# Softcap attention feeding a max-of-two-projections layer: the matmul order inside g, the place of quad 0's first attention-times-V, and the place of w1 - w2

## The chip, the cores and the metric

The kernel runs on one core of one Trainium2 chip. The time is the device time of one execution in microseconds (us), taken as the median over several executions. Before the change it is 378.27 us (13 runs, 377.13 to 380.69).

The core has four engines that matter here, each with its own in-order instruction stream: TensorE (PE) does matrix products and writes them into PSUM banks; VectorE (DVE) copies results out of PSUM and does elementwise work; ScalarE (ACT) does tanh and exp; GpSimd (POOL) does casts, one multiply, and starts some transfers. SyncE (SP) only issues transfers. An instruction that waits holds up everything behind it on its own engine.

## The reference: what is computed

Inputs are q, k and v of shape (8 batches, 12 heads, 448 positions, 64), and the weights w1, w2 (768 x 1024) and w_out (1024 x 768), all in float32.

```python
scores = scale * q @ k.T            # per batch and head, scale = 1/8
scores = cap * tanh(scores / cap)   # cap = 30
attn   = exp(scores - max) / (sum(exp(scores - max)) + 1e-9)
x      = attn @ v                   # heads side by side: 3584 tokens x 768
out    = maximum(x @ w1, x @ w2) @ w_out
```

## The kernel before, in words

**Algebra.** Because |scores| is at most 30, the row maximum is not subtracted. The maximum of the two projections is rewritten: max(x w1, x w2) = x w2 + relu(x (w1 - w2)). So the kernel forms `wd` = w1 - w2 (`wd_sb`) and `wm` = w2 w_out (`wm_sb`) once, and each batch then needs g = relu(x wd) and out = x wm + g w_out. All matrix products are in bf16.

**Attention, in quads.** A pair is two heads of one batch, and there are 48 pairs. A quad t is two consecutive pairs i = 2t and 2t + 1, so there are 24 quads and three quads make a batch. For each quad: `scores(t, p)` (lines 277 to 298) does the products of k and q of part p = 0..3 on PE, into one of two double-bank `s` tiles, followed by tanh on ACT; `ex(t, p)` (line 300) is the exp on ACT; `pv(t, ab)` (line 330) is attention times v for one of the two pairs: seven matmuls into the one `pv` bank, then a copy to `u` by DVE (line 356). `pv(t, 1)` also adds up the exponentials into the `ss` bank (lines 345 and 352), which DVE copies to `st` and SP sends out for the reciprocals. The bank pool of `pv` has one buffer, so a `pv` can't start before the `u` copy of the one before is done. Later come `invert` (reciprocal, line 368), `spread` (transfer of the reciprocals to all partitions, `rec_b`, line 376) and `normalize` (POOL multiplies `u` by `rec_b` into `xT`, line 388). `xT` has six chunks per batch, one per pair; chunks 4 and 5 are from the batch's last quad.

**Setting up.** `transposes(i)` turns the early k and q on PE, and DVE copies them (line 264). `cast(nc.vector, 0, "v")` puts group 0's v into bf16 `vp` on DVE (lines 151 and 155). The rows of w2 are turned on PE (line 221) and multiplied by w_out (line 232). `subtract(c)` (line 214) makes chunk c of `wd_sb` on DVE from a chunk of w1 (`w1_in`, three buffers in the `osb` pool, loaded by `load_w1`) and w2.

**The filler.** Everything that is not attention runs as generators in the list `fill_q`: each `yield` follows one matmul, and `F(n)` lets the first generators advance n matmuls. The main loop over quads (line 534 on) strews `F(n)` between the attention steps, so PE always has work between two score products. The order on every engine is written out by hand in this way: the kernel turns the scheduler off with `tc.manual_schedule()`, and the order of the emission is the order of the instructions. After the last quad the rest of the filler runs alone.

**One batch of the layer** is the generator `moe(b)` (line 397 on). The first part computes g in eight blocks f = 0..7 of 128 columns; each block is six matmuls (chunks c = 0..5 of `xT`, line 405) into one bank of the `mm` pool, which has two banks, and then one relu copy by DVE (line 410). The second part is the output in tiles of 128 tokens and half rows: six matmuls with `wm_sb` (line 418), eight with `wo_sb` (line 421), and a copy to `osb` (line 425). Both parts take turns on the same two `mm` banks. In the kernel before, blocks 0 and 1 are done together: chunks 0 to 3 of block 0, chunks 0 to 3 of block 1, then chunks 4 and 5 of block 0, then chunks 4 and 5 of block 1. Blocks 2 to 7 follow one at a time.

Of the kernel before, what the change touches and what calls it, by code (L numbers as in the profile page):

```python
# [10 lines left out]
def kernel(  # L11
# [11 lines left out]
    nc = tc.nc  # L23
# [9 lines left out]
    P = 128  # L33
# [277 lines left out]
    def add(t, ab, step):  # L311

        if t < NS or t >= NQ:
            return
        if t not in esum:
            esum[t] = att.tile([P, 4, S], bf16, name="esum")
        d = esum[t][:, 2 * ab : 2 * ab + 2, :]
        if step == 2:

            r = slice(64 * ab, 64 * ab + 64)  # L320
            d = esum[t][r, ab::2, :]
            nc.vector.tensor_add(d, d, expo[t, 2][r, :, :])  # L322
        elif step == 0:
            nc.vector.tensor_add(d, e_of(t, ab, 1 if ab else 0), e_of(t, ab, 2 if ab else 1))  # L324
        else:
            nc.vector.tensor_add(d, d, e_of(t, ab, 0 if ab else 2))  # L326
# [3 lines left out]
    def pv(t, ab):  # L330


        i = 2 * t + ab
        g, n = divmod(i, L)
        ps = pv_psum.tile([P, 512], f32, name="pv")
        for j in range(NJ):
            for h in range(2):
                r = slice(64 * h, 64 * h + 64)
                nc.tensor.matmul(  # L339
                    ps[r, :S], vp[g % 2][:, 2 * n + h, j, :], e_of(t, ab, j)[:, h, :], start=(j == 0), stop=False  # L340
                )
        if ab:
            ss = pv_psum.tile([P, 512], f32, name="ss")
            for m in range(2 if t < NS else 0):
                nc.tensor.matmul(
                    ss[64 * m : 64 * m + 64, :S], ones2, expo[t, 2][:, m, :], start=True, stop=False
                )
            nj = NJ if t < NS else 1
            for j in range(nj):
                for m in range(4):  # L350
                    x = e_of(t, m // 2, j)[:, m % 2, :] if t < NS else esum[t][:, m, :]
                    nc.tensor.matmul(ss[32 * m : 32 * m + 32, :S], ones, x, start=(t >= NS), stop=(j == nj - 1))  # L352
        nc.tensor.matmul(ps[:, :S], vl[g % 2][:, n, :], expo[t, 2][:, ab, :], start=False, stop=True)  # L353
        if ab == 0:
            U[t] = upool.tile([P, 2, S], f32, name="u", bufs=4)
        nc.vector.tensor_copy(U[t][:, ab, :], ps[:, :S])  # L356
        if ab:
            st = upool.tile([P, S], f32, name="st", bufs=1)
            nc.vector.tensor_copy(st, ss[:, :S])

            sums[t] = xpool.tile([32, 56], f32, name="sums")
            nc.sync.dma_start(
                out=sums[t], in_=st.rearrange("(m p) (a c) -> m p a c", p=32, a=8)[:, 0, :, :]
            )
# [28 lines left out]
    def moe(b):  # L393
        if b % 2 == 0:
            gT[b // 2] = xpool.tile([P, FC, 2 * S], bf16, name="gT", bufs=1)
        g, x = gT[b // 2], xT[b // 2]
        cs = slice((b % 2) * S, (b % 2 + 1) * S)

        psg = {f: mm_psum.tile([P, 512], f32, name="mm") for f in range(2)}
        order = [(f, c) for cc in (range(4), range(4, KC)) for f in range(2) for c in cc]  # L400
        order += [(f, c) for f in range(2, FC) for c in range(KC)]
        for f, c in order:
            if f not in psg:
                psg[f] = mm_psum.tile([P, 512], f32, name="mm")
            nc.tensor.matmul(  # L405
                psg[f][:, :S], wd_sb[:, c, f * P : (f + 1) * P], x[:, c, cs], start=(c == 0), stop=(c == KC - 1)
            )
            yield
            if c == KC - 1:
                nc.vector.tensor_relu(g[:, f, cs], psg[f][:, :S])  # L410
        for t in range(3) if b % 2 == 0 else range(3, 7):
            osb = opool.tile([P, DF], f32, name="osb")[:, :DM]
            ts = slice(t * P, (t + 1) * P)
            for half in range(2):
                hs = slice(half * (DM // 2), (half + 1) * (DM // 2))
                ps = mm_psum.tile([P, 512], f32, name="mm")
                for c in range(KC):
                    nc.tensor.matmul(ps[:, : DM // 2], x[:, c, ts], wm_sb[:, c, hs], start=(c == 0), stop=False)  # L418
                    yield
                for f in range(FC):  # L420
                    nc.tensor.matmul(  # L421
                        ps[:, : DM // 2], g[:, f, ts], wo_sb[:, f, hs], start=False, stop=(f == FC - 1)
                    )
                    yield
                nc.vector.tensor_copy(osb[:, hs], ps[:, : DM // 2])  # L425
                if b == B - 1 and t == 6:
                    o = out[b * S : b * S + NJ * P, hs].rearrange("(p j) n -> p j n", j=NJ)
                    nc.sync.dma_start(out=o[:, NJ - 1, :], in_=osb[:, hs])
            if b == B - 1 and t == 6:
                continue  # L430
            wide = b * NP >= NT * L
            if t == 3:
                for n in range(2):
                    o = out[(b - 1 + n) * S : (b + n) * S, :]
                    to = o[NJ * P : S, :] if wide else o.rearrange("(r j) n -> r j n", j=R7)[:, R7 - 1, :]
                    nc.sync.dma_start(out=to, in_=osb[64 * n : 64 * n + 64, :])
            else:
                j = t if t < 3 else t - 4
                o = out[b * S : (b + 1) * S, :]
                if wide:  # L440
                    nc.sync.dma_start(out=o[: NJ * P, :].rearrange("(p j) n -> p j n", j=NJ)[:, j, :], in_=osb)
                else:
                    o = o.rearrange("(r j) n -> r j n", j=R7)
                    for n in range(2):
                        nc.sync.dma_start(out=o[:, 2 * j + n, :], in_=osb[64 * n : 64 * n + 64, :])
# [3 lines left out]
    def F(n):  # L449
        while n > 0 and fill_q:  # L450
            try:
                next(fill_q[0])
                n -= 1
            except StopIteration:
                fill_q.pop(0)
# [78 lines left out]
    for t in range(NQ):  # L534
        i = 2 * t
        more = t + 1 < NQ
        more8 = 1 if t >= 8 and more else 0
        weights(i)
        if t % 3 == 2 and t > 5:
            fill_q.append(moe(t // 3 - 1))  # L540
        if more:
            scores(t + 1, 0)
        ex(t, 3)
        F(2)
        add(t, 0, 1)
        F(2)
        if i + 3 < NT * L:
            transposes(i + 3)
        if t == 0:
            cast(nc.vector, 0, "v")  # L550
        F(4 + more8 if more else 0)
        if t == 4:
            normalize(t - 2, 0)
            normalize(t - 2, 1)
        if t in crosses:
            cross(crosses[t])
        if t > 4:
            spread(t - 2)
        extra(i)
        F(5 + 2 * more8 if more else 3)  # L560
        if more:
            scores(t + 1, 1)
            ex(t + 1, 0)
        pv(t, 0)
        F(4)
        add(t, 1, 0)
        F(3 + more8 if more else 4)
        F(3 if more else 0)
        if 3 <= i < 3 + KC:
            subtract(i - 3)  # L570
        if t > 4:
            normalize(t - 2, 0)
            normalize(t - 2, 1)
        if more:
            scores(t + 1, 2)
            ex(t + 1, 1)
        weights(i + 1)
        if t == 4:
            fill_q.append(moe(0))
        if i + 4 < NT * L:  # L580
            transposes(i + 4)
        add(t, 0, 2)
        F(2 + more8 if more else 2)
        add(t, 1, 2)
        F(4 + more8 if more else 3)
        add(t, 1, 1)
        F(2 if more else 8)
        if 1 < t < 4:
            spread(t - 2)
        if t > 2:  # L590
            invert(t - 1)
        extra(i + 1)
        F(2 + more8 if more else 0)
        if more:
            scores(t + 1, 3)
            ex(t + 1, 2)
        if t == 3:
            spread(t - 1)
        pv(t, 1)
        F(4)  # L600
        if more:
            add(t + 1, 0, 0)
        F(3 if more else 0)
        if 0 < t < 3:
            invert(t - 1)
        if 1 < t < 4:
            normalize(t - 2, 0)
            normalize(t - 2, 1)
        if 3 <= i + 1 < 3 + KC:
            subtract(i - 2)  # L610
    F(6)
    spread(NQ - 2)
    F(10)
# [43 lines left out]
```

## Time and profile before

| | |
|---|---|
| median of 13 runs | 378.27 us (377.13 to 380.69) |
| the profiled execution's own time | 377.69 us |
| its span on the core | 375.9 us |
| PE busy | 343.3 us, 91% |
| ACT busy | 281.7 us, 75% |
| DVE busy | 231.0 us, 61% |
| POOL busy | 160.9 us, 43% |
| matmuls of g (line 405) | 384 |
| relu copies (line 410) | 64, 38.8 us in all |

The span is the time from the first to the last instruction; the 1.8 us by which the execution's own time is longer lie around it. In the lists of instructions below, the columns are the start in us from the span's start, the length in us, the engine, the line, the operation with its output and inputs, the shape, and how many instructions are merged; in square brackets stands the idle time of the engine just before, with what ended it. In the lists of waits, the columns are the engine and line that waited, what it waited for, the total in us, how often, and the longest.

### The profile page before, as it was taken

The numbers are of one execution on the slowest core, as the hardware profiler recorded it, in microseconds if no ns is written. First come the engines' busy times: TensorE is split into PE (matmuls) and PEld (weight loads), VectorE is DVE, ScalarE is ACT, GpSimd is POOL, SyncE is SP. The second block draws the span as 40 slices with busy tenths as digits, with TensorE's granted clock in tenths as the row PEclk, the third lists the DMA queues.
The fourth block names the chain that finished last, engine by engine and source line by source line (L and its number), as shares of the span: only waits on it lengthen the run. The fifth ranks groups of instructions, "written<-read, shape, count | busy, mean of one in ns | idle before, by whom it ended". The sixth has DMA issues, their size and how long they took to land.

```text
span 375.9 us, 6501 instructions
## 1 busy us (share of the span) xinstructions
PE 343.3 (91%) x2454; PEld 164.5 (44%) x2454; DVE 231.0 (61%) x389; ACT 281.7 (75%) x265; POOL 160.9 (43%) x197
## 2 busy tenths in 40 slices
PE   4667897899999999989999999989998999999996
PEld 2224344444444444434453445434443445455563
DVE  4163567576776776767775767577666968433421
ACT  4979998798999999987998899978996892000000
POOL 4770079592664356308433942384415222220000
PEclk9999999999999999999999999999999999999999
DMA  7999899758799969688799889999866034512022
GB/s 245 340 234 216 319 263 277 138 141 210 191 234 234 246 179 242 189 206 235 203 224 242 219 213 228 218 269 212 235 151 188 8 91 136 143 44 84 0 85 84
DMA packets 101200, 71.56 MB, mean 190 GB/s; under 512 B 56496, under 2 KB 96176, under 8 KB 101168
## 3 DMA queue, kind: packets, MB, share of 16 engines
q1 hardware_dynamic: 99216, 67.99, 68.7%
q0 software_dynamic: 1952, 3.15, 4.5%
q8 instruction: 19, 0.31, 0.3%
q14 instruction: 13, 0.11, 0.1%
HBM read 53.48 MB, written 11.18 MB: 172 GB/s over the span
## 4 chain that ended last, share of the span: by engine, by line
PE 71%; DVE 13%; ACT 11%; issue 2%; DMA 2%; SPq 0%; POOL 0%; DVEq 0%; ACTq 0%
PE mm L421 17%; PE mm L405 16%; PE mm L418 13%; PE pv L339 8%; PE s L295 7%; ACT expo L303 5%; ACT tanh L296 5%; PE pv L353 3%; PE ss L352 2%; PE mm L232 2%; DMA kr<-in_k_dram 2%; PE s L290 2%; DVE gT L410 2%; DVE u L356 1%; DVE esum L324 1%
## 5 line engine op out<-in xcount | busy, mean ns | idle before, releaser
L303 ACT ACTIVATE expo<-tanh 128x1792 bf16<-128x1792 bf16 (+1 forms) x96 | 144.8, 1509 | 0.1
L296 ACT ACTIVATE tanh<-s 128x896 bf16<-128x896 f32 x144 | 124.2, 914 | 24.6 <-PE s L295 23.1
L388 POOL TENSOR_TENSOR xT<-u,rec_b 128x448 bf16<-128x448 f32 x48 | 60.9, 1289 | 132.1 <-DMA rec_b<-rec_d 101.6
L405 PE MATMUL mm<-xT,wd_sb 128*128 128x448 bf16 x384 | 80.9, 352 | 7.6 <-DVE gT L410 5.5
L421 PE MATMUL mm<-wo_sb,gT 128*128 128x384 bf16 x448 | 85.3, 326 | 0.0
L356 DVE COPY u<-pv 128x448 f32<-128x448 f32 x48 | 30.0, 625 | 75.8 <-PE pv L353 75.8
L418 PE MATMUL mm<-wm_sb,xT 128*128 128x384 bf16 x336 | 66.9, 326 | 0.2 <-DVE gT L410 0.2
L405 PEld LDWEIGHTS <-wd_sb 128*128 128x128 bf16 x384 | 36.9, 98 | 45.2 <-issue 14.2
L421 PEld LDWEIGHTS <-gT 128*128 128x128 bf16 x448 | 43.4, 98 | 30.0 <-issue 2.2
L295 PE MATMUL s<-qkT 64*128 64x448 bf16 x288 | 43.5, 370 | 7.9 <-ACT tanh L298 3.1
L425 DVE COPY osb<-mm 128x384 f32<-128x384 f32 x56 | 31.0, 553 | 28.6 <-PE mm L421 28.2
L410 DVE TENSOR_SCALAR gT<-mm 128x448 bf16<-128x448 f32 x64 | 38.8, 618 | 14.7 <-PE mm L405 14.4
L418 PEld LDWEIGHTS <-xT 128*128 128x128 bf16 x336 | 32.5, 98 | 23.5 <-issue 1.9
L339 PE MATMUL pv<-expo,vp 128*64 128x448 bf16 x288 | 37.5, 365 | 3.2 <-DVE vp L151 3.2
L326 DVE TENSOR_TENSOR esum<-esum,expo 128x896 bf16<-128x896 bf16 x38 | 30.7, 808 | 1.7
L324 DVE TENSOR_TENSOR esum<-expo 128x896 bf16<-128x896 bf16 x38 | 28.0, 736 | 0.0
L322 DVE TENSOR_TENSOR esum<-esum,expo 64x896 bf16<-64x896 bf16 x38 | 26.9, 708 | 0.7
L298 ACT ACTIVATE tanh<-s 128x896 bf16<-128x896 f32 x24 | 22.0, 916 | 5.7 <-PE s L290 5.1
L295 PEld LDWEIGHTS <-qkT 64*128 64x128 bf16 x288 | 9.8, 95 | 33.5 <-issue 29.0
L339 PEld LDWEIGHTS <-vp 128*64 128x64 bf16 x288 | 12.4, 109 | 24.7 <-issue 15.5
L232 PE MATMUL mm<-wo_sb,w2T 128*128 128x384 bf16 x96 | 18.4, 326 | 4.5 <-DVE qkT L264 4.5
L151 POOL CAST vp<-vr 64x576 bf16<-64x576 f32 x12 | 8.9, 738 | 20.5 <-PE s L295 17.6
(59 smaller groups left out, 251.9 us busy)
## 6 DMA issues: line engine op xcount, KB each, us to landing
rec_b<-rec_d SPq DMA_DIRECT2D x48, 224.0 KB
kr<-in_k_dram SPq DMA_DIRECT2D x12, 576.0 KB
qr<-in_q_dram SPq DMA_DIRECT2D x12, 576.0 KB
vr<-in_v_dram SPq DMA_DIRECT2D x12, 576.0 KB
out_dram<-osb SPq DMA_DIRECT2D x17, 384.0 KB
out_dram<-osb SPq DMA_DIRECT2D x22, 192.0 KB
osb<-in_moe_w_dram SPq DMA_DIRECT2D x6, 512.0 KB
vr<-in_v_dram SPq DMA_DIRECT2D x4, 672.0 KB
```

The source lines that it names most:

```text
L295: nc.tensor.matmul(s[:, h, :S], k0[r, j * P : (j + 1) * P], qTn[r, :])
L296: nc.scalar.activation(tanh[t, p][:, 2 * m : 2 * m + 2, :], s[:, :, :S], AF.Tanh, scale=scale / cap)
L303: nc.scalar.activation(expo[t, p], tanh[t, p][:, 0:n, :], AF.Exp, scale=float(cap))
L324: nc.vector.tensor_add(d, e_of(t, ab, 1 if ab else 0), e_of(t, ab, 2 if ab else 1))
L339: nc.tensor.matmul(ps[r, :S], vp[g % 2][:, 2 * n + h, j, :], e_of(t, ab, j)[:, h, :], start=(j == 0), stop=False)
L356: nc.vector.tensor_copy(U[t][:, ab, :], ps[:, :S])
L388: eng.tensor_mul(xT[b // 2][:, hp, cs], U[t][:, ab, :], rec[t][:, ab, :])
L405: nc.tensor.matmul(psg[f][:, :S], wd_sb[:, c, f * P : (f + 1) * P], x[:, c, cs], start=(c == 0), stop=(c == KC - 1))
L410: nc.vector.tensor_relu(g[:, f, cs], psg[f][:, :S])
L418: nc.tensor.matmul(ps[:, : DM // 2], x[:, c, ts], wm_sb[:, c, hs], start=(c == 0), stop=False)
L421: nc.tensor.matmul(ps[:, : DM // 2], g[:, f, ts], wo_sb[:, f, hs], start=False, stop=(f == FC - 1))
L425: nc.vector.tensor_copy(osb[:, hs], ps[:, : DM // 2])
```

## The change

Three edits.

1. In `moe`, the eight blocks of g are each done in one go: six matmuls, then the relu copy, for f = 0 to 7. The pairing of blocks 0 and 1 is gone.
2. `pv(0, 0)`, the first attention times v of all, is put off: it no longer stands after part 1 of quad 1's scores but after part 3, just ahead of `pv(0, 1)`. All other quads keep their order.
3. Three of the six `subtract` calls (chunks 0, 2 and 4) move from the end of quads 1, 2 and 3 into the next quad, behind its first scores, an exp and two filler matmuls.

```diff
-        psg = {f: mm_psum.tile([P, 512], f32, name="mm") for f in range(2)}
-        order = [(f, c) for cc in (range(4), range(4, KC)) for f in range(2) for c in cc]
-        order += [(f, c) for f in range(2, FC) for c in range(KC)]
-        for f, c in order:
-            if f not in psg:
-                psg[f] = mm_psum.tile([P, 512], f32, name="mm")
-            nc.tensor.matmul(
-                psg[f][:, :S], wd_sb[:, c, f * P : (f + 1) * P], x[:, c, cs], start=(c == 0), stop=(c == KC - 1)
-            )
-            yield
-            if c == KC - 1:
-                nc.vector.tensor_relu(g[:, f, cs], psg[f][:, :S])
+        for f in range(FC):
+            ps = mm_psum.tile([P, 512], f32, name="mm")
+            for c in range(KC):
+                nc.tensor.matmul(
+                    ps[:, :S], wd_sb[:, c, f * P : (f + 1) * P], x[:, c, cs], start=(c == 0), stop=(c == KC - 1)
+                )
+                yield
+            nc.vector.tensor_relu(g[:, f, cs], ps[:, :S])
...
         ex(t, 3)
         F(2)
+        if 3 < i <= 3 + KC:
+            subtract(i - 4)
         add(t, 0, 1)
...
             scores(t + 1, 1)
             ex(t + 1, 0)
-        pv(t, 0)
+        if t > 0:
+            pv(t, 0)
         F(4)
...
             scores(t + 1, 3)
             ex(t + 1, 2)
+        if t == 0:
+            pv(t, 0)
         if t == 3:
             spread(t - 1)
         pv(t, 1)
...
             normalize(t - 2, 0)
             normalize(t - 2, 1)
-        if 3 <= i + 1 < 3 + KC:
-            subtract(i - 2)
```

## The prediction

> **What bounds the kernel now.** I read the 40 slices and the chain first, then the waits of PE, then PE's and DVE's instructions around each place that the change touches.
>
> ```profile
> PE   4667897899999999989999999989998999999996
> ACT  4979998798999999987998899978996892000000
> ...
> PE 71%; DVE 13%; ACT 11%; issue 2%; DMA 2%; SPq 0%; POOL 0%; DVEq 0%; ACTq 0%
> ```
>
> A slice is 9.4 us. From 80 us on PE is full, ACT nearly so up to about 310 us, and then PE works alone. So a PE wait after 80 us costs time, provided ACT, which PE feeds, has idle time of its own there. PE's waits after 80 us (total, times, longest):
>
> ```profile
> PE mm L405 <- DVE gT L410: 5.5, 9, 1.4
> PE mm L405 <- DVE osb L425: 1.4, 3, 1.0
> PE mm L405 <- DVE wm_sb L237: 0.6, 1, 0.6
> PE s L295 <- ACT tanh L298: 0.5, 1, 0.5
> PE s L295 <- ACT tanh L296: 0.5, 2, 0.3
> ```
>
> Nearly all are matmuls of g (L405) waiting for DVE to empty an `mm` bank. The same list for ACT has 16.9 us of waits for PE's scores after 80 us (L296 14.3, L298 2.6), so ACT follows when PE gets faster.
>
> The last batch shows the wait alone, with nothing else running:
>
> ```profile
> 344.48 2.49 PE L405 MATMUL mm<-xT,wd_sb 128*128 128x448 bf16 x12
> 347.30 6.97 PE L405 MATMUL mm<-xT,wd_sb 128*128 128x448 bf16 x36 [0.34 <-DVE gT L410]
> ```
>
> The 36 matmuls take 6.97 us with a last length of 0.35, so they start every (6.97 - 0.35)/35 = 0.189 us. Twelve should bring block 2 to 344.48 + 12 x 0.189 = 346.75; it starts at 347.30. The price is 0.55, not the 0.34 of idle time: a matmul's drawn length of 0.352 hides 0.16 of each wait. Over the 13 waits for banks the price is 5.5 + 1.4 + 0.6 + 13 x 0.16 = 9.6 us.
>
> **Edit 1: blocks of g in one go.** No instruction is added or removed. Before, blocks 0 and 1 end only two matmuls apart (0.38 us), and block 2 needs the bank of block 0 just then, while its relu copy takes 0.62. After, block 2 comes six matmuls (1.13 us) behind block 0's end. That this distance suffices on a free DVE is seen in the 36: blocks 2 to 7 follow each other at six matmuls with no wait. Also, block 1 asks for its bank two matmuls (0.38) later, so the waits for `osb` and `wm_sb` shrink by up to 0.38.
>
> The largest wait, in batch 2 (PE, then DVE):
>
> ```profile
> 162.95 0.92 PE L405 MATMUL mm<-xT,wd_sb 128*128 128x448 bf16 x4
> 164.12 1.29 PE L405 MATMUL mm<-xT,wd_sb 128*128 128x448 bf16 x6 [0.25 <-DVE osb L425]
> 167.02 0.54 PE L405 MATMUL mm<-xT,wd_sb 128*128 128x448 bf16 x2
> 168.97 1.10 PE L405 MATMUL mm<-xT,wd_sb 128*128 128x448 bf16 x5 [1.40 <-DVE gT L410]
> ```
>
> ```profile
> 167.22 0.62 DVE L356 COPY u<-pv 128x448 f32<-128x448 f32 x1 [2.10 <-PE pv L353]
> 167.76 0.61 DVE L359 COPY st<-ss 128x448 f32<-128x448 f32 x1
> 168.30 1.15 DVE L410 TENSOR_SCALAR gT<-mm 128x448 bf16<-128x448 f32 x2
> ```
>
> Both relu copies stand behind `u` and `st` of an attention step. After, block 0 ends near 164.1, and in DVE's new order its copy stands ahead of `u`, in the 2.10 us of idle time. Block 1 starts at 164.12 as before (the bank comes free then) but has only four matmuls left to do ahead of the scores, not six: 0.38 gained. Block 2 then follows at 167.4 - 0.38 = 167.02 rather than 168.97: 1.95 in all. Block 3 needs block 1's copy, third in DVE's queue, done at 168.5 and wanted at 168.6.
>
> Worked likewise from each batch's rows:
> - Batch 0: block 1 still waits for `wm_sb` to 83.87; block 2 at 83.87 + 1.13 = 85.00, its copy done at 85.06 (behind an `esum`), against 85.88: 0.82.
> - Batch 1: 124.92 becomes 124.35 (copy in the place of an `esum` at 123.72): 0.57.
> - Batch 3: `osb` wait (0.21) and gT wait (0.34) both go; 203.42 becomes 202.55: 0.87.
> - Batch 4: block 2 from 248.03 to 246.80, but block 1's copy now stands behind an `esum` of 1.37 (the neighbours without POOL beside them take 0.61), so block 3 waits to about 248.45 against 249.16: 0.71 is left. This is what is late next.
> - Batch 5: the waits of 1.21 and 0.46 become one, since block 2's copy still stands behind two slow `esum` (1.02 and 1.37); block 4 at 287.25 against 288.04: 0.79.
> - Batches 6 and 7: 0.55 each.
>
> Sum 6.8 us. The upper bound is all 9.6. The lower is the two last batches alone in full and half of the other 5.7, if ACT or DVE holds PE instead: 1.1 + 2.85 = 3.95.
>
> **Edit 2: pv(0, 0) put off.**
>
> ```profile
> 23.92 1.33 PE L339 MATMUL pv<-expo,vp 128*64 128x448 bf16 x5 [1.83 <-DVE vp L151]
> 25.53 0.95 PE L290 MATMUL s<-qkT 128*128 128x448 bf16 x2
> 28.22 0.76 PE L339 MATMUL pv<-expo,vp 128*64 128x448 bf16 x6
> ```
>
> ```profile
> 26.58 0.92 ACT L298 ACTIVATE tanh<-s 128x896 bf16<-128x896 f32 x1 [2.44 <-PE s L290]
> ```
>
> PE waits for DVE's casts of v, and the scores behind that (L290) leave ACT idle for 2.44 us. After, these scores need only a free `s` bank (21.7), so tanh follows the exp at 24.14: ACT gains 2.44 there. The next wait: PE does the second scores of part 3 at 25.0 (behind that tanh) to 25.5, then pv(0, 0), 1.61 (23.92 to 25.53), to 27.1. The one `pv` bank must be emptied: 0.25 + 0.62 for `u`, to 27.97. Then pv(0, 1) and its sums, 1.87 (28.22 to 30.09) at the speed they had, to 29.85; and quad 2's first scores behind them, 0.37, to 30.2. Queued behind the new wait is all of PE. Tanh of quad 2 began at 31.71, so 1.5 is left of 2.44.
>
> PE is slow here, though: 26 transposes take 0.90 at 26.42 and 0.60 at 31.52, both at a granted clock of 1.00, and the switch shows only after 23.92 to 27.8 without a gap. The new order has gaps at 24.0 to 25.0 and 27.1 to 28.0, so pv(0, 1) is likely slow too: 1.87 x 1.5 = 2.8, and the scores end at 31.3. Gain 0.4. If the slowness also reaches the 1.3 us of turning w2 and transposes at 31.2, it costs 0.6 and the edit loses 0.2 or more. I take +0.5, bounds -0.6 and +1.5, nearer the slow rows because of the gaps. ACT's gain passes on to PE: between 28 and 40 us PE waits 2.9 us for tanh.
>
> [...]
>
> **Edit 3: w1 - w2 moved.** Nothing. In the order of instructions on each engine, all six subtractions keep their places in DVE's stream: between a quad's end and the third line of the next, DVE gets nothing else. SP's, POOL's and ACT's streams are the same, row by row, so no DMA, load of w1 or cast moves. The only DVE rows out of place are five relu copies and the `u` of pv(0, 0), all told above. Cost 0, bounds 0 and 0.
>
> **Sum.** 6.8 + 0.5 + 0 = 7.3 us off the profiled execution's 377.69: 370.4. The median of the runs stands 0.6 above that execution, so **371.0 us**.
>
> **Rivals.**
> - *ACT holds PE.* The waits go, but PE then waits for tanh; only the stretch after 318 us, without ACT, gains: 1.1 + 0.5 = 1.6, 376.7 us. Against: ACT has its own waits in just these places, such as 2.09 us at 170.47 and 1.90 at 285.87.
> - *The wait moves on to block 3*, since DVE is what is late: 378 us. For: batches 4 and 5. Against: the 36 matmuls without a wait, and the idle DVE ahead of `u` in batches 2, 3 and 5.
> - *Chunks 4 and 5 come too late, and it gets slower.* Block 0 now wants chunk 5 as sixth matmul, not tenth. POOL makes that chunk just ahead in batches 1 and 3:
>
> ```profile
> 119.43 1.52 POOL L388 TENSOR_TENSOR xT<-u,rec_b 128x448 bf16<-128x448 f32 x1
> 197.40 1.14 POOL L388 TENSOR_TENSOR xT<-u,rec_b 128x448 bf16<-128x448 f32 x1
> ```
>
> It ends at 120.95 and 198.54; PE wants it at 122.9 and 200.85. The margins are 1.95 and 2.3. The other batches have over 4. To end slower, both must lose 7.3 + 1.1 = 8.4 together, so `rec_b` must land 6.3 us later than shown; at 7 us it is 377.69 + 9.75 - 7.3 + 0.6 = 380.7. For: POOL waits up to 9.9 us for `rec_b`. Against: that chain starts from the same PE stream and moves with it.
> - *All bank waits vanish and pv gives its best*: 9.6 + 1.5 = 11.1, 367.2 us.
>
> **How the numbers follow.** Forecast 0.80, from 368 to 375: 375 is both lower bounds together (3.95 - 0.6 = 3.35 off 378.3), 368 is a gain of 10.3, 0.8 short of both upper bounds. Everything gone 0.05; ACT 0.06; wait moves on 0.05; slower 0.04. The range of 368 to 375 leaves 0.2 outside. About 0.3% (1.1 us) is what a measurement of this kernel can tell from no change. Faster: 0.80 + 0.05 + 0.04 of the ACT case = 0.89; same 0.07; slower 0.04.
>
> **What the new profile would show.** Right: the waits of L405 for gT fall from 5.5 to under 2 us, none in the last two batches, whose 48 matmuls run in one piece; ACT's 2.44 before L298 goes and a shorter one appears at quad 2's first tanh; L214 keeps its neighbours. Wrong: L405 waiting for POOL's `xT`, longer waits of L295 for tanh after 80 us, or 26 transposes still at 0.90 after 32 us.

## The result and the profile after

The changed kernel takes 372.7 us (median of 11 runs, 371.18 to 375.3) against 378.17 us (48 runs of the kernel before in the same session). The ratio is 0.9855, with a 95% interval of 0.9833 to 0.9877: 5.5 us faster, with a 95% interval of 4.7 to 6.3. The forecast was 371.0 (368 to 375), a gain of 7.3.

The profiled execution took 373.17 us, with a span of 371.4. The busy tenths of PE and ACT and the chain of the page after (a slice is now 9.3 us):

```profile
PE   3668898899999999999999999999999999999996
ACT  3996997899999989998889899988997993000000
...
PE 74%; DVE 10%; ACT 7%; DMA 7%; issue 1%; SPq 1%; POOL 0%; DVEq 0%; ACTq 0%; POOLq 0%
```

PE is still the bound. It is busy 344.2 us, as before (343.3), in a span shorter by 4.5. Its share of the chain rose from 71% to 74%, and transfers, which had 2%, now have 7% (the longest piece of it is the transposing transfer `qkT<-kqf`, 7.65 us at 186.47; before, it was a load of k, 3.98 us). PE's waits after 80 us in the changed kernel (total, times, longest):

```profile
PE mm L401 <- DVE gT L405: 1.4, 2, 0.9
PE s L295 <- DMA qkT<-kqf: 0.8, 1, 0.8
PE mm L401 <- DVE osb L420: 0.6, 1, 0.6
PE mm L413 <- DVE gT L405: 0.5, 2, 0.3
...
PE ss L352 <- DVE esum L326: 0.2, 1, 0.2
PE mm L401 <- DVE wm_sb L237: 0.2, 1, 0.2
```

The first edit makes this part of the file shorter by four lines at the matmul and five behind it, so L401 is the matmul of g (L405 before), L405 its relu copy (L410), L413 the first output matmul (L418), L416 the second (L421) and L420 the copy to `osb` (L425). The wait for the relu copies fell from 5.5 us in nine pieces to 1.4 us in two, and the waits for `osb` and `wm_sb` shrank from 1.4 and 0.6 to 0.6 and 0.2. Two lines are new: scores that wait for a transfer (`qkT<-kqf`), and sums that wait for `esum`; the wait of L413 grew from 0.2 to 0.5. ACT follows: its waits for scores after 80 us fell from 16.9 us to 12.5 (L296 10.8, L298 1.7).

The last batch, in the list of PE's instructions of the changed kernel (columns as in the prediction):

```profile
340.50 9.24 PE L401 MATMUL mm<-xT,wd_sb 128*128 128x448 bf16 x48
```

All 48 matmuls of g stand in one piece of 9.24 us. Before, they took from 344.48 to 354.27, which is 9.79. The gain of 0.55 is the price that the start-to-start spacing gave, not the 0.34 of idle time that was drawn. Batch 2, which had the largest wait:

```profile
163.04 2.08 PE L401 MATMUL mm<-xT,wd_sb 128*128 128x448 bf16 x10
165.06 0.55 PE L295 MATMUL s<-qkT 64*128 64x448 bf16 x4
...
166.73 1.49 PE L401 MATMUL mm<-xT,wd_sb 128*128 128x448 bf16 x7
...
173.14 2.25 PE L401 MATMUL mm<-xT,wd_sb 128*128 128x448 bf16 x11
```

Blocks 0 and 1 are 12 matmuls: the ten of the first row and the first two of the seven at 166.73. Block 2 follows in the same seven, and the wait of 1.40 that stood in front of it is gone.

The start, where the second edit acts, in the changed kernel: PE, then ACT.

```profile
26.30 1.33 PE L339 MATMUL pv<-expo,vp 128*64 128x448 bf16 x6
...
28.84 1.33 PE L339 MATMUL pv<-expo,vp 128*64 128x448 bf16 x6 [0.72 <-DVE u L356]
...
30.47 1.31 PE L352 MATMUL ss<-expo,ones 128*32 128x448 bf16 x12
...
32.20 0.93 PE L295 MATMUL s<-qkT 64*128 64x448 bf16 x4
...
33.60 0.90 PE L262 MATMUL mm<-ident,kqf 64*64 64x64 bf16 x26
```

```profile
24.84 0.92 ACT L298 ACTIVATE tanh<-s 128x896 bf16<-128x896 f32 x1
...
32.85 1.73 ACT L296 ACTIVATE tanh<-s 128x896 bf16<-128x896 f32 x2 [2.91 <-PE s L295]
```

ACT's 2.44 us of idle time in front of L298 is gone, as forecast. But 2.91 us, more than was saved, now stand in front of quad 2's first tanh. PE ran everything between 26.3 and 34.5 at its slow lengths: six `pv` matmuls take 1.33 us, not 0.76; four scores 0.93, not 0.55; the 26 transposes 0.90, not 0.60. From quad 1's first tanh to quad 2's, 14.22 us became 14.69.

### The profile page after: what moved, and what is told of

The parts are those of the page before. It is cut to its first block, busy times and chain, and to the rows that moved or that the text cites. A ratio compares the mean times of both kernels' runs of the same rounds, so it can differ in the third digit from the quotient of the medians.

```text
span 371.4 us, 6501 instructions
## 1 busy us (share of the span) xinstructions
PE 344.2 (93%) x2454; PEld 165.0 (44%) x2454; DVE 233.8 (63%) x389; ACT 281.6 (76%) x265; POOL 162.4 (44%) x197
## 4 chain that ended last, share of the span: by engine, by line
PE 74%; DVE 10%; ACT 7%; DMA 7%; issue 1%; SPq 1%; POOL 0%; DVEq 0%; ACTq 0%; POOLq 0%
PE mm L416 18%; PE mm L401 16%; PE mm L413 13%; PE pv L339 8%; PE s L295 7%; PE pv L353 3%; ACT tanh L296 3%; ACT expo L303 3%; DMA kr<-in_k_dram 3%; PE mm L232 2%; PE ss L352 2%; DMA qkT<-kqf 2%; PE s L290 2%; DVE u L356 2%; DVE esum L324 1%; DVE gT L405 1%
## 5 line engine op out<-in xcount | busy, mean ns | idle before, releaser
L296 ACT ACTIVATE tanh<-s 128x896 bf16<-128x896 f32 x144 | 124.2, 914 | 24.6 <-PE s L295 22.8
L416 PE MATMUL mm<-wo_sb,gT 128*128 128x384 bf16 x448 | 85.3, 326 | 0.0
L401 PE MATMUL mm<-xT,wd_sb 128*128 128x448 bf16 x384 | 79.5, 352 | 2.3 <-DVE gT L405 1.4
L413 PE MATMUL mm<-wm_sb,xT 128*128 128x384 bf16 x336 | 66.9, 326 | 0.5 <-DVE gT L405 0.5
L416 PEld LDWEIGHTS <-gT 128*128 128x128 bf16 x448 | 43.4, 98 | 30.0 <-issue 2.2
L401 PEld LDWEIGHTS <-wd_sb 128*128 128x128 bf16 x384 | 37.0, 98 | 37.7 <-issue 6.0
L420 DVE COPY osb<-mm 128x384 f32<-128x384 f32 x56 | 30.9, 552 | 30.6 <-PE mm L416 30.3
L405 DVE TENSOR_SCALAR gT<-mm 128x448 bf16<-128x448 f32 x64 | 39.4, 616 | 11.1 <-PE mm L401 10.8
L413 PEld LDWEIGHTS <-xT 128*128 128x128 bf16 x336 | 32.5, 98 | 24.0 <-issue 2.6
L326 DVE TENSOR_TENSOR esum<-esum,expo 128x896 bf16<-128x896 bf16 x38 | 29.7, 782 | 1.6
L324 DVE TENSOR_TENSOR esum<-expo 128x896 bf16<-128x896 bf16 x38 | 30.6, 806 | 0.0
L322 DVE TENSOR_TENSOR esum<-esum,expo 64x896 bf16<-64x896 bf16 x38 | 28.9, 759 | 0.7
L298 ACT ACTIVATE tanh<-s 128x896 bf16<-128x896 f32 x24 | 22.0, 916 | 2.4 <-PE s L290 1.7
L151 POOL CAST vp<-vr 64x576 bf16<-64x576 f32 x12 | 9.8, 821 | 21.3 <-PE s L295 17.6
```

Of the source, the lines that this page charges most:

```text
L296: nc.scalar.activation(tanh[t, p][:, 2 * m : 2 * m + 2, :], s[:, :, :S], AF.Tanh, scale=scale / cap)
L401: nc.tensor.matmul(ps[:, :S], wd_sb[:, c, f * P : (f + 1) * P], x[:, c, cs], start=(c == 0), stop=(c == KC - 1))
L405: nc.vector.tensor_relu(g[:, f, cs], ps[:, :S])
L416: nc.tensor.matmul(ps[:, : DM // 2], g[:, f, ts], wo_sb[:, f, hs], start=False, stop=(f == FC - 1))
```

## The experiments

Two theories stood against each other on where the missing 1.8 us (7.3 less 5.5) went. The first: the second edit costs, because PE falls into its slow lengths. The second: the first edit gives less than 6.8, because transfers hold PE once the bank waits are gone. Each ratio below is to the kernel before on the same chip; that kernel had 378.42 us beside the three runs of one edit alone and the run with loads ahead, and 378.26 beside the other four, which ran on another chip.

### The first edit alone

```diff
-        order = [(f, c) for cc in (range(4), range(4, KC)) for f in range(2) for c in cc]
...
+        for f in range(FC):
+            ps = mm_psum.tile([P, 512], f32, name="mm")
+            for c in range(KC):
```

> Only the blocks of g in one go; pv(0, 0) and w1 - w2 stand as before. Theory (the whole gain is the blocks, pv(0, 0) put off costs some 0.5 us at the start because its PE work stays slow): 372.2 us or a little less, about 6 us (1.6%) off the kernel before; L401-type waits for gT fall from 5.5 us to about 1.5. Rival (the prediction's step: pv put off gains 0.5): 373.2 us, slower than the changed kernel by 0.5.

Measured: 0.9817 (0.979 to 0.9844), 371.74 us. This is 6.9 us, with an interval of 5.9 to 7.9, against the 6.8 of the forecast. By the medians the first edit is worth more alone than all three together; the two intervals (0.979 to 0.9844 and 0.9833 to 0.9877) overlap a little. PE's waits after 80 us in this kernel:

```profile
PE mm L401 <- DVE gT L405: 1.7, 2, 1.4
PE s L295 <- DMA qkT<-kqf: 1.2, 2, 0.8
```

The wait for the transfer is here too, so the second and third edits did not bring it.

### The second edit alone

```diff
-        pv(t, 0)
+        if t > 0:
+            pv(t, 0)
...
             ex(t + 1, 2)
+        if t == 0:
+            pv(t, 0)
```

> Only pv(0, 0) put off. Theory: quad 2's first tanh starts about 0.5 us later against quad 1's first tanh than before (14.2 us apart before), PE's 26 transposes still take 0.90 us near 33 us; time 378.2 to 378.8, no gain. Rival (the prediction's step): 0.5 us faster, 377.7; that tanh 13.7 us after quad 1's first.

Measured: 1.0029 (1.0006 to 1.0052), 379.54 us. It loses 1.1 us (0.2 to 2.0). PE at the place, then ACT:

```profile
29.69 1.31 PE L352 MATMUL ss<-expo,ones 128*32 128x448 bf16 x12
```

```profile
32.07 1.73 ACT L296 ACTIVATE tanh<-s 128x896 bf16<-128x896 f32 x2 [2.92 <-PE s L295]
```

This is what the changed kernel shows, too: a slow 1.31 us for 12 sums, and 2.92 us of idle time on ACT. The gap between the two tanh is 14.69 us, the same to the hundredth. The two edits alone add up to 6.9 - 1.1 = 5.8, and all three together gave 5.5, so nothing else is needed to account for the total, within intervals that are each about 2 us wide.

### The third edit alone

```diff
+        if 3 < i <= 3 + KC:
+            subtract(i - 4)
...
-        if 3 <= i + 1 < 3 + KC:
-            subtract(i - 2)
```

> Only w1 - w2 moved. By the order of instructions no engine gets anything in another place, so 378.2 us, within what two runs of one kernel differ (0.3%). Rival (the subtraction blocked DVE at quad ends): 1 us or more faster.

Measured: 0.9982 (0.9952 to 1.0013), 378.35 us. No difference, as forecast.

### PE kept busy across the gaps of the second edit

If the slow lengths are the cause, useless work in the gaps must help. This kernel has the second edit, keeps g's blocks paired as before, and adds ten matmuls of the identity with `qkT`, whose product nobody reads.

```diff
+    def keep_busy(n):
+        ps = mm_psum.tile([P, 512], f32, name="mm")
+        for _ in range(n):
+            nc.tensor.matmul(ps[:, :S], ident, ...)
...
+        if t == 0:
+            keep_busy(4)
...
-            scores(t + 1, 3)
+            scores(t + 1, 3, 0, 1)
+            if t == 0:
+                keep_busy(3)
+            scores(t + 1, 3, 1, 2)
...
+        if t == 0:
+            pv(t, 0)
+            keep_busy(3)
```

> pv(0, 0) put off as in the change, blocks of g as before, and ten matmuls that nobody reads fill PE's three gaps between 20 and 28 us (4 ahead of the scores of part 2, 3 between the two scores of part 3, 3 between pv(0, 0) and pv(0, 1)). Theory (PE's slow phase lasts longer because of these gaps): the matmuls after pv(0, 0) run at the fast length (26 transposes 0.60, the 12 of ss 0.75), quad 2's first tanh comes 0.7 us or more earlier than with pv put off alone (14.7 after quad 1's first there). Rival (the order alone is what costs): the matmuls stay slow or the tanh comes no earlier. Total 377.5 by the theory, 379.5 by the rival.

Measured: 0.9954 (0.9926 to 0.9982), 376.26 us. Ten matmuls that compute nothing turn a loss of 0.29% into a gain of 0.46%. PE in this kernel, then ACT (L527 is the useless work):

```profile
27.05 0.73 PE L527 MATMUL mm<-qkT,ident 128*128 128x448 bf16 x3
...
28.80 0.75 PE L352 MATMUL ss<-expo,ones 128*32 128x448 bf16 x12
...
30.59 0.60 PE L262 MATMUL mm<-ident,kqf 64*64 64x64 bf16 x26
```

```profile
30.25 1.73 ACT L296 ACTIVATE tanh<-s 128x896 bf16<-128x896 f32 x2 [0.47 <-PE s L295]
```

The 12 sums take 0.75 instead of 1.31, the transposes 0.60 instead of 0.90, and ACT waits 0.47 us instead of 2.92. The gap between the two tanh is 12.25 us, 2.44 less than with the edit alone. So with this order the edit gains in the way the forecast described only when PE gets to its short lengths in time. No run here fills the gaps in the changed kernel as a whole.

### The first pv put off by one step only

In the kernel before, `pv(0, 0)` waits for the casts of v. If that is the whole of what a delay can save, a shorter one should do: behind part 2 of the scores, not part 3. This kernel has the first edit and this delay, and leaves the subtractions where they were.

```diff
-        pv(t, 0)
+        if t > 0:
+            pv(t, 0)
...
             scores(t + 1, 2)
             ex(t + 1, 1)
+        if t == 0:
+            pv(t, 0)
```

> Blocks of g in one go, and pv(0, 0) put off by one step only: behind quad 1's scores of part 2, not of part 3. Then its seven matmuls start when v is cast, and the u copy hides under transposes and the scores of part 3. Theory (putting pv off far serialises pv(0, 0), its copy and pv(0, 1) ahead of quad 2's scores, and that is what it loses): quad 2's first tanh 12.5 to 13.5 us after quad 1's first (before 14.2, changed kernel 14.7); time 370 to 371.5, against 371.7 with the blocks alone. Rival (any shift at the start is taken up again by the transfers' pace after 80 us): the same 371.7 as with the blocks alone.

Measured: 0.9762 (0.973 to 0.9794), 369.46 us: 9.0 us off, faster than both kernels. PE and ACT:

```profile
22.89 1.33 PE L339 MATMUL pv<-expo,vp 128*64 128x448 bf16 x6
...
33.86 0.56 PE L290 MATMUL s<-qkT 128*128 128x448 bf16 x2 [1.18 <-ACT tanh L296]
34.35 0.90 PE L262 MATMUL mm<-ident,kqf 64*64 64x64 bf16 x26
```

```profile
24.42 0.92 ACT L298 ACTIVATE tanh<-s 128x896 bf16<-128x896 f32 x1
...
29.55 1.73 ACT L296 ACTIVATE tanh<-s 128x896 bf16<-128x896 f32 x2
```

Neither tanh has idle time in front of it. `pv(0, 0)` starts at 22.89, and the copy of its bank lies beside the transposes and scores that follow, so `pv(0, 1)` finds the bank empty. The gap between the two tanh is 11.81 us. PE is still slow in the first `pv` (1.33), and slow again in the transposes at 34.35; the two scores at 33.86, right behind the wait of 1.18, still took the short 0.56. The tanh at 29.55 lies between these two spells. The short delay was run only together with the first edit. By the medians it adds some 2 us to that, but the intervals (0.973 to 0.9794 here, 0.979 to 0.9844 there) touch, so its own worth is not measured closely.

### The loads ahead of the reciprocals

This bears on the one rival that ended slower: that chunks 4 and 5 of `xT` come too late. Its margins were 1.95 and 2.3 us, and nothing of it shows in the changed kernel. The run was expected to show something else, whether SP's turn makes `qkT` late, but it makes `rec_b` late, and so shows what that rival costs. In the changed kernel the prefetch of the next inputs is put on SP's queue ahead of `spread`, not behind it.

```diff
-        if t > 4:
-            spread(t - 2)
         extra(i)
+        if t > 4:
+            spread(t - 2)
```

> The changed kernel with one more edit on SP's queue: in each quad from 5 on, the loads of k, q or v are issued ahead of the spread of the reciprocals (rec_b), not behind. SP waits up to 4.9 us for rec_d before it issues rec_b, and the loads, the next sums and the transposing transfer of qkT stand behind that. Theory (SP's turn sets when qkT is ready, and this holds PE's gain back): the transposing transfers start up to 3 us earlier, the 0.82 us wait of PE's scores for qkT goes, time 371.2 to 371.9. Rival 1 (the transfer engines' throughput sets it): the transposing transfers start as in the changed kernel, time 372.7. Rival 2 (rec_b later makes POOL's multiplies and the casts behind them late): 373.5 or more.

Measured: 0.9952 (0.9927 to 0.9976), 376.79 us, some 4 us slower than the changed kernel, as its second rival had it. The wait for `qkT` is gone from PE's list all the same. POOL in batch 1, then PE:

```profile
122.92 2.22 POOL L388 TENSOR_TENSOR xT<-u,rec_b 128x448 bf16<-128x448 f32 x2 [3.60 <-DMA rec_b<-rec_d]
```

```profile
124.10 0.35 PE L401 MATMUL mm<-xT,wd_sb 128*128 128x448 bf16 x1 [2.51 <-POOL xT L388]
125.84 3.84 PE L401 MATMUL mm<-xT,wd_sb 128*128 128x448 bf16 x11
```

`rec_b` lands behind the loads, and these chunks begin at 122.92, not 118.34 as in the kernel before: 4.58 us late. The matmul that waits is the fifth of block 0, which wants chunk 4. In the kernel before chunk 4 is done at 119.47, and the fifth matmul of the batch starts at 121.25: a margin of 1.78, tighter than the 1.95 that the forecast gave for chunk 5. Less this margin, the matmul should start 2.8 us later than there; it starts at 124.10, 2.85 later. So the mechanism is real, and block 0 done in one go does need the margin; in the changed kernel only 0.82 us of it is left (chunk 4 done at 120.34, its matmul at 121.16). A little after the wait, 11 matmuls take 3.84 us; the changed kernel did such 11 in 2.25 (its row at 173.14). So the slow lengths behind the wait took another 1.59 us.

### The output stores taken off SP's queue

The second theory: PE waits for `qkT<-kqf` because SP issues it late, behind output stores. In the changed kernel PE meets this wait once, in batch 3:

```profile
179.70 0.37 PE L352 MATMUL ss<-esum,ones 128*32 128x448 bf16 x2 [0.24 <-DVE esum L326]
...
194.16 0.55 PE L295 MATMUL s<-qkT 64*128 64x448 bf16 x4 [0.82 <-DMA qkT<-kqf]
```

That transfer was issued at 186.47, against 186.36 in the kernel before, although PE ran 1.24 us ahead by then. From 146 to 261 us these transposing transfers start within 0.3 us of their old times. (With the first edit alone they start 0.7 to 1.6 us earlier than before, but they were 1.3 us ahead already at 82 us.) So two kernels were made from the first edit alone: one with the stores of batches 0 to 5 on POOL's queue, and one without these stores.

```diff
-  nc.sync.dma_start(out=..., in_=osb...)
+  (nc.gpsimd if b < 6 else nc.sync).dma_start(out=..., in_=osb...)
```

> Blocks of g in one go; the output stores of batches 0 to 5 are issued on POOL's queue, not SP's. The bytes moved stay. Theory (SP's issuing, some 0.6 us each, one after the other, sets when the transposing transfers of qkT start): they start 1 us or more earlier from 140 us on, PE's wait of 0.8 us for qkT near 193 us goes, time 370.5 to 371.2. Rival 1 (the transfer engines' throughput sets it): no earlier, 371.7. Rival 2 (POOL waits for osb ahead of its multiplies and casts): 373 or more, with PE waiting for xT or qkT.

Measured: 0.99 (0.9861 to 0.9939), 375.05 us, 3.3 us slower than the first edit alone. POOL's waits, then PE's after 80 us:

```profile
POOL out_dram L431 <- DVE osb L420: 13.0, 3, 10.5
POOL out_dram L436 <- DVE osb L420: 10.1, 4, 4.3
```

```profile
PE mm L401 <- DVE gT L405: 3.6, 5, 1.9
PE mm L401 <- DVE osb L420: 1.4, 2, 0.8
```

A store on POOL's queue waits for its `osb` copy, up to 10.5 us, and POOL's multiplies and casts stand behind it. The bank waits on PE doubled. This kernel shows the cost of a wait on POOL, and says little about SP.

```diff
+            if b < 6:
+                continue
             wide = ...
```

> Blocks of g in one go; the output stores of batches 0 to 5 are left out (those batches' results stay unwritten). Both SP's time and the bytes are taken away: this bounds what relief of the transfers is worth. Theory (transfers hold back a part of PE's gain): PE's wait for qkT goes and time falls to 370 or below. Rival (DVE and ACT hold it): 371.7 within 0.3%.

Measured: 0.9826 (0.9783 to 0.9869), 372.26 us, level with the first edit alone (0.9817). PE's waits after 80 us keep the bank wait and have no line for the transfer:

```profile
PE mm L401 <- DVE gT L405: 1.5, 3, 0.7
```

The transfers had room (between 156 and 200 us their engines were busy 0.81 of the time, against 0.89 with the first edit alone), the wait went, and the time stayed. But the interval of this run is 3.3 us wide, so the removed 0.8 us could not have shown by itself, and its profile has a slow spell of PE (35.90 to 39.31) that the profile of the first edit alone does not have. What speaks against the second theory is the first edit alone: it gave 6.9 of the 6.8 forecast. That transfers cost nothing is not shown: in the profile of the first edit alone they are 17% of the chain, with one transposing transfer of 8.98 us at 145.29, against 2% in the kernel before. How much they hold back stays open.

## Why the prediction was right or wrong

**What bounds the kernel: right.** PE's waits after 80 us were worth their price, ACT had slack and followed.

**Edit 1: right in size, 6.8 forecast and 6.9 measured alone.** The start of the same matmul in both traces gives the terms one by one. Gained in batches 0 to 3: 0.80, 0.54, 1.94 and 0.58 (forecast 0.82, 0.57, 1.95, 0.87); in batches 4 and 5: 1.13 and 1.39 (0.71 and 0.79); in the last two together 1.07 (1.1). That is 7.45 in this pair of traces. Against it stand three losses that the forecast did not have, 0.72 + 0.61 + 0.88 = 2.2 us. The first is a relu copy behind a slow `esum` in batch 1 of the changed kernel (DVE, then PE):

```profile
131.46 1.40 DVE L324 TENSOR_TENSOR esum<-expo 128x896 bf16<-128x896 bf16 x1
132.78 0.61 DVE L405 TENSOR_SCALAR gT<-mm 128x448 bf16<-128x448 f32 x1
```

```profile
133.45 1.29 PE L401 MATMUL mm<-xT,wd_sb 128*128 128x448 bf16 x6 [0.56 <-DVE gT L405]
```

The forecast saw this pattern in batch 4, in front of block 3, and called it "what is late next". It did not come there, which is why batch 4 gained more; it came in batch 1, in front of block 7. The second of the two gT waits that remain is where the forecast left one, in front of block 4 of batch 5 (0.89 at 284.82). The other two losses are the waits at 179.70 and 194.16 shown above. The net of this pair is 5.25. But traces of the same order of work scatter by 1 to 2 us. From quad 2's tanh (L298) to quad 23's, the four traces that keep the blocks paired have 267.8, 267.9, 269.5 and 269.9 us, and four with the blocks in one go (leaving out the two runs that changed queues) have 262.5, 263.2, 263.2 and 265.1. The means, 268.8 and 263.5, differ by 5.3, and with the last two batches' 1.1 that makes 6.4, near the 6.9 of the timed run (one of the four is the kernel without stores). The split over batches is that of one execution. That the total came out so close is partly luck: batches 4 and 5 gave 2.52 where 1.50 was forecast, and the three waits that the forecast put at nothing took 2.2.

**Edit 2: wrong, with the wrong sign.** The failed step is "the scores end at 31.3. Gain 0.4", and with it "I take +0.5, bounds -0.6 and +1.5". The measured -1.1 lies below even the lower bound of -0.6, though its interval (-0.2 to -2.0) reaches above it. Two things were mis-sized.

- The factor of slowness. The forecast took 1.5, from transposes of 64 columns. The sequence from `pv(0, 1)` to the scores took 3.36 us (28.84 to 32.20) instead of 1.87, a factor of 1.8, and the four scores behind it 0.93 instead of 0.55. The slowness also reached the transposes at 33.60. The forecast had named that case, "it costs 0.6 and the edit loses 0.2 or more", and did not take it. By starts, the way in which it priced the bank waits, the factor for 448 columns is 1.97: in the slow spell of the run with loads ahead these matmuls start every 0.373 us (125.84 to 128.83), otherwise every 0.189; a short row hides part of this in the length of its last matmul (one alone, L353, takes 0.55 at 27.57 in the changed kernel and 0.36 at 29.79 in the kernel before, a factor of 1.5). The spell also lasts longer. The first matmul of 448 columns at a short length starts at 26.3 to 29.1 us in the five profiles with the old order of `pv`, at 33.6 to 34.9 in the three with `pv(0, 0)` put off, at 25.9 with the useless matmuls and at 27.6 with the short delay.
- The baseline. The forecast compared with one start. From quad 0's tanh of part 2 (L298) to quad 2's, the profiled execution of the kernel before took 24.88 us, but four others with the old order took 23.50, 24.05, 23.89 and 24.30. They differ by DVE's casts of v: from the start of the first cast to `vp` to the end of the last it took 4.46 us in the first, and 3.05, 3.61, 3.47 and 3.87 in the others; what is left is 20.42 to 20.45 in all five. The mean is 24.1. With `pv(0, 0)` put off, all three traces have 25.36. So the typical loss is 1.2, which the timed run confirms with 1.1, while the pair of profiles alone shows 0.47. The bounds were worked out against the slowest of five starts, and so were too kind to the edit.

In these traces the short lengths return behind a stretch of work without a drawn gap: in the changed kernel they are there at 34.94, with no gap since 28.84; with the useless matmuls at 25.86, with none since 20.56, and 1.31 became 0.75; in the kernel with the short delay after about 5 us (22.05 to 27.3) and after 3.9 (33.86 to 37.76). How long a stretch it takes is not shown. The slow lengths at 34.35 in that last kernel came after idle times of 0.43 and 1.18 us with work between them. The loss of 0.2 that the forecast named and did not take was nearer than its +0.5, and still short of the measured 1.1.

**Edit 3: right.** Nothing, 0.9982 with 1 inside the interval.

**The rivals.** ACT did not hold PE; its waits shrank. The wait did not move on to block 3 anywhere. Late chunks did not occur, but the run with loads ahead shows that the mechanism is real; the forecast overlooked that chunk 4, with 1.78 us, is tighter than chunk 5. Of the signs that the forecast listed as showing it wrong one appeared, 26 transposes at 0.90 after 32 us, and it pointed to the edit that was wrong. Of the signs of being right one failed: the idle time at quad 2's first tanh came longer (2.91), not shorter, than the 2.44 that went. Waits for `xT` and longer waits for tanh did not appear.

**The sum.** 7.3 forecast, 5.5 measured: 6.8 against 6.9, +0.5 against -1.1, and 0 against 0. The range was wide enough for this because it held both lower bounds together.

## What to carry to other kernels

With two PSUM banks, price a bank wait by the spacing of matmul starts, not by the drawn idle time, and ask how many matmuls lie between a block's end and the reuse of its bank: here six (1.13 us) hide a 0.62 us copy and two (0.38 us) do not. Put a step off only until its input is ready; one step further made its neighbour wait 0.72 us for the same bank (28.84 in the changed kernel). Ahead of any edit that makes new gaps on PE, look for rows of the same matmul with two lengths, and check more than one execution before a baseline of a start is believed.

## What the runs showed of the hardware that was not expected

- PE's drawn rows change by 1.5 (26 transposes, 0.60 to 0.90) to 1.75 (12 sums 0.75 to 1.31; 6 `pv` 0.76 to 1.33), and the spacing of 448-column matmuls by 1.97 (0.189 to 0.373), while the row of the granted clock in the profile of the changed kernel shows nine tenths or more in every slice.
- The slow lengths can come back after short waits: in the kernel with the short delay (a wait of 1.18 us at 33.86; 26 transposes took 0.60 at 29.62 and 0.90 at 34.35), and after 2.51 us at 124.10 in the kernel with loads ahead, where 11 matmuls cost 3.84 us instead of 2.25. They did not begin right behind the wait (six `pv` at 124.86 still took 0.76), and each spell lasted 3.3 to 3.4 us (34.35 to 37.76, 125.84 to 129.14). Nor do they always come: with the first edit alone, waits of 0.44 and 1.19 us at 32.18 and 34.72 left the transposes at 35.19 at 0.60. What decides is open.
- Useless work on PE can pay: ten matmuls that nobody reads moved the ratio from 1.0029 to 0.9954.
- A drawn wait of 0.24 us in front of two sums (L352) moved PE by 0.61 us against the trace of before, more than the "idle plus 0.16" that held for the matmuls of g.
- An `esum` of 128 rows (L324, L326) took 0.61 to 0.63 us in the changed kernel where no row of POOL lay beside it, and up to 1.58 (at 258.90) beside POOL's casts and multiplies, though not each time (0.62 at 225.74, beside a cast). The one of 1.40 at 131.46, with a POOL cast from 131.24 to 132.39, stood just ahead of the relu copy that became the next wait.
